# Attention block on one core: q of the twelve plain units given out up to two units sooner, the first quad's y twice a unit

## The chip, the cores and the metric

The kernel runs on one core of a Trainium2 chip. The metric is the device time in microseconds (us), of the slowest core where there are several; here it is the one core. Kernels are compared by medians of runs on the same chip.

The engines are named as in the profile: PE is the matrix engine (TensorE), PEld its weight loads, DVE is VectorE, ACT is ScalarE, POOL is GpSimd, SP is the engine from which all the DMAs of the main part are issued. Each engine takes its instructions strictly in the order in which the program lists them.

## What is computed

A block with adaptive layer norm, attention with 32 query heads over 8 key/value heads and the last 512 positions of a cache, and a gated feed-forward part. Cut to what matters here (the feed-forward part comes after the stretch that the change touches):

```python
def _A_ref(x, k_cache, v_cache, wq, wo):
    W = min(4096, max(256, Sk // 4))          # 512
    q = (x @ wq).reshape(B, Sq, Hq, Dh)       # 2048 rows, 32 heads of 128
    k = jnp.repeat(k_cache[:, :, Sk - W:, :], rep, axis=1)
    v = jnp.repeat(v_cache[:, :, Sk - W:, :], rep, axis=1)
    scores = jnp.einsum("bhqd,bhkd->bhqk", q, k) * (Dh ** -0.5)
    p = _softmax(scores, axis=-1)
    o = jnp.einsum("bhqk,bhkd->bhqd", p, v)
    return o.reshape(B, Sq, Hq * Dh) @ wo

mod = (_silu(c) @ w_mod).reshape(c.shape[0], 6, 1, -1)
h = _layernorm(x, axis=-1) * (1 + ca) + sa
x = x + ga * _A_ref(h, A_k_cache, A_v_cache, A_wq, A_wo)
h = _layernorm(x, axis=-1) * (1 + cb) + sb
x = x + gb * _B_ref(h, B_w_gate, B_w_up, B_w_down)
```

## The kernel before

**Precision.** Every float32 operand of a product is split into two float16 halves, a high and a low one, and each product is three matmuls (low by high, high by high, high by low) into one float32 bank: the helper `mm3` at L91 issues nearly all the matmuls of the program. A split is made in two instructions: the high half as a copy with a cast (on ACT or POOL), the low half as the difference (on DVE or POOL).

**Units and steps.** The attention goes by units: one head of one block of 512 query rows. Four units (two heads by two row blocks) form a group g, which shares one pair of heads `pr`; two pairs share one key/value head (a quad of heads). A unit has four steps t, each for 128 query rows: unit u holds steps 4u to 4u+3. A step of the main loop issues, in this order:

- PE: the scores `ps` of step t, three matmuls, into one of two banks (a third score tile can start only when the exponential of two steps before has read its bank);
- DVE: the row maximum `nm` of `ps`; ACT: the exponential `ee` from `ps` and `nm` into a tile of its own, with the row sums;
- ACT: the high half `p` of step t-2; DVE: the low half `p` of step t-3, behind which SP issues the DMA that turns both halves (`pt<-p`, a DMA transpose);
- PE: up to three groups of three matmuls, popped from a list `work`, or from a second list `ywork` when the first is empty.

Step 0 is the first `ps` of the profile; the steps below are counted by the groups of three `ps` matmuls.

**What the lists hold.** At the first step of each unit u, `pushes(u, y)` adds to `work`: the product of probabilities and V of unit u-2 (`po`, four groups, which need all four turned tiles of unit u-2), the q product of a coming unit, and, from unit 12 on, output products `y` (`py`: o by wo of a finished quad of heads, four groups for 128 rows, added to the running sum by DVE). For the first three groups of units (g < 3, units 0 to 11, "plain") q of unit u+1 is one product of four groups (`pq`). From g = 3 on the q of a group of four units is made by a scheme with seven products instead of eight (`qa`, `qb`, `qc`), spread over the four units before; its operands are combinations of the weights, which POOL makes as a set (`w0`, `w1`, `w2`, `x3`). Where a step finds both lists empty, PE has only the three `ps` matmuls there.

**Small work with a due step.** Loads, statistics and weight preparation are put on a table by step. `sched(pos, (load, steps))` sets the step at which a preparation runs and lets its load be issued up to three steps sooner, when its buffer is free; `at(("w", t), fn)` runs a function at the end of step t. A pair of weight tiles `rw` goes through two buffers (`NRW` = 2): the next pair's load waits until the previous pair has been converted. For each pair of weights ACT takes a sum of squares (`junk<-rw`), PE sums it over the partitions (`pst`), and POOL and DVE make scales of it; K has the same statistic (`junk<-raw`). Plain weights of the third pair are split by ACT and DVE, those of the second pair by POOL. These statistics stand in ACT's list between the exponentials.

**Where the change is.** `turned_out`, `get_qt` and `yt_turn` take tiles from the ring "qt"; the loop over g at L1233 and below sets the due steps; `pushes` builds the PE list; the main loop at its end adds `y`. The number of buffers of "qt" is written as 3 in three places.

Of the kernel before, what the change touches and what calls it, by code (L numbers as in the profile page):

```python
# [48 lines left out]
GW = 3  # L49
# [3 lines left out]
NPT = 3  # L53
NE = 6
CB = (11, 27)
PSE = dict.fromkeys((5, 7, 8, 9, 14, 18, 19, 21, 22, 23, 25, 26, 27), "acc") | dict.fromkeys((11, 15, 20, 24, 28), "qa")
# [9 lines left out]
def block_kernel(ctx: ExitStack, tc: tile.TileContext, x, kT, v, wq, wo, wg, wu, wd, cT, wc, wm, out):  # L66
# [500 lines left out]
    def turned_out(qb, dt):  # L567
        tag, n = (("qt", 3), ("v16", 2))[dt % 2]
        f = pool.tile([P, D], F32, tag=tag, name="hf", bufs=n)
        v = f.rearrange("p (t q) -> p t q", t=QT)  # L570
        sc = cols[:, 4, dt:dt + 1]
        nc.scalar.activation(v, TURN[qb][:, :, dt, :], AF.Identity, scale=sc, bias=cols[:, 3, dt:dt + 1])
        put_off(2, lambda: nc.vector.scalar_tensor_tensor(v, TURN[qb][:, :, KT + dt, :], sc, v, op0=ALU.mult, op1=ALU.add))
        put_off(4, lambda: dma(spilled(3, qb)[:, dt, :], f))
# [59 lines left out]
    def get_qt():  # L634
        return pair("qt", "qt", 3)

# [598 lines left out]
    for g in range(NG):  # L1235
# [6 lines left out]
        if 0 < g < GW:  # L1242
            a, b = plain_steps(g, by)
            sched_pair(g, srcs, t0 - (19 if g > 1 else 13), spread, [(t0 - (12 if g > 1 else 8), a)], [(t0 - (8 if g > 1 else 7), b)])
        elif g >= GW and (not half or pr < GW):
# [14 lines left out]
        else:  # L1260
            if g > 0:
                if pr % 2 == 0:
                    load, stat, spread_, parts = k_items(pr)
                    sched(t0 - (22 if g > 2 else 20), (load, [stat]))
                    at(("w", t0 - (19 if g > 2 else 17)), spread_)
                load, stat, spread_, parts = k_items(pr)
# [284 lines left out]
    def pushes(u, y):  # L1551
# [11 lines left out]
        if g < GW:  # L1563
            w = q_plain(u + 1) if 0 < u + 1 < 4 * GW else []
            if u + 1 == 4 * GW:
                return nxt[2] + nxt[6] + pv + nxt[7]
            return w + pv + (nxt[1] if nxt and k == 2 else [])
        f = items(g)
# [9 lines left out]
    with tc.manual_schedule():  # L1578
        begin()
        nexty, invs = [], {}  # L1580
        for t in range(T + TAIL):
            now[0] = t
            u, s = divmod(t, 4)
            if s == 0:
# [3 lines left out]
                work += pushes(u, y)  # L1588
            if s == 2 and (t >= T or u < GW * 4) and nexty:
                ywork += nexty.pop(0)  # L1590
# [137 lines left out]
    def yt_turn(g, c, qb):  # L1728

        def split():  # L1730
            tag, bufs = (("qt", 3), ("v16", 2))[YR.get("n", 0) % 2]
            u = YR["u", c, qb] = pool.tile([P, 2, QB], U16, tag=tag, name="yu", bufs=bufs)
# [128 lines left out]
```

## Time and profile before

| | us |
|---|---|
| median of 3 runs | 1726.62 |
| lowest and highest | 1725.72, 1727.48 |
| span of the profiled execution | 1724.3 |
| PE busy in it | 1705.4 |
| DVE busy | 1424.2 |
| ACT busy | 1257.4 |
| POOL busy | 1088.1 |

The span runs from the first to the last instruction of one profiled execution. The time of that execution is not listed apart; the difference of its span to the median of the runs is 2.3 us, for what lies before the first and behind the last instruction.

How the views are read: the page gives the busy time of each engine. The list of waits says which engine waited for whom, in total, how often, and the longest. The table of windows gives, for a stretch of the span, the busy time of PE, PEld, DVE, ACT and POOL with the count of instructions, the clock granted to PE, the busy share of the DMA engines and their GB/s. The timeline gives the start, the length, the engine, the line, the operation and what it writes and reads, a count, and in square brackets the idle time before it. The end of a matmul is modelled: a single one is shown as 0.38 us long while the next may start much sooner, so PE's pace is read from starts. SPq rows are DMAs as SP issues them; the length is that of the issue, and the list of DMA issues says how long after the issue they land.

### The profile page before, as it was taken

The numbers are of one execution on the slowest core, as the hardware profiler recorded it, in microseconds if no ns is written. First come the engines' busy times: TensorE is split into PE (matmuls) and PEld (weight loads), VectorE is DVE, ScalarE is ACT, GpSimd is POOL, SyncE is SP. The second block draws the span as 40 slices with busy tenths as digits, with TensorE's granted clock in tenths as the row PEclk, the third lists the DMA queues.
The fourth block names the chain that finished last, engine by engine and source line by source line (L and its number), as shares of the span: only waits on it lengthen the run. The fifth ranks groups of instructions, "written<-read, shape, count | busy, mean of one in ns | idle before, by whom it ended". The sixth has DMA issues, their size and how long they took to land.

```text
span 1724.3 us, 26250 instructions
## 1 busy us (share of the span) xinstructions
PE 1705.4 (99%) x7961; PEld 780.0 (45%) x7961; DVE 1424.2 (83%) x2480; ACT 1257.4 (73%) x2823; POOL 1088.1 (63%) x1322
## 2 busy tenths in 40 slices
PE   7999999999999999999999999999999999999999
PEld 4344444444444444444444444444444444444444
DVE  8888888888888999888888888888896788676666
ACT  7988788888878877888778777788785354455442
POOL 3879777776788884655665755757760345735424
PEclk9999999999999999999999999999999999999999
DMA  7999999999999998999999999899997556365353
GB/s 242 222 207 214 214 217 205 226 202 227 213 217 236 201 212 181 212 211 225 216 220 222 211 227 206 198 236 212 222 232 162 164 144 195 121 165 174 99 158 102
DMA packets 693454, 343.51 MB, mean 199 GB/s; under 512 B 579136, under 2 KB 602688, under 8 KB 693312
## 3 DMA queue, kind: packets, MB, share of 16 engines
q1 hardware_dynamic: 693024, 341.30, 85.3%
q8 instruction: 63, 1.03, 0.3%
q14 instruction: 79, 0.65, 0.1%
q10 hardware_dynamic: 288, 0.52, 0.1%
HBM read 137.50 MB, written 63.70 MB: 117 GB/s over the span
## 4 chain that ended last, share of the span: by engine, by line
PE 92%; ACT 4%; DVE 2%; DMA 2%; issue 1%; SPq 0%; ACTq 0%; DVEq 0%
PE py L91 20%; PE po L91 18%; PE ps L91 17%; PE fa L91 8%; PE qa L91 8%; PE fc L91 4%; PE qc L91 4%; PE ya L91 4%; PE qb L91 2%; PE fb L91 2%; PE yc L91 2%; ACT ee L1009 1%; ACT p L1021 1%; PE yb L91 1%; DMA rw<-in_wq 1%
## 5 line engine op out<-in xcount | busy, mean ns | idle before, releaser
L1009 ACT ACTIVATE ee<-ps,nm 128x512 f32<-128x512 f32 x512 | 349.7, 683 | 185.3 <-DVE nm L1000 182.7
L1026 DVE SCALAR_TENSOR_TENSOR p<-ee,rr,p 128x512 f16<-128x512 f32 x512 | 454.4, 888 | 8.5 <-ACT p L1021 8.0
L1000 DVE TENSOR_REDUCE nm<-ps 128x1 f32<-128x512 f32 x512 | 350.1, 684 | 96.8 <-PE ps L91 94.9
L91 PE MATMUL ps<-k,qt 128*128 128x512 f16 x1536 | 414.7, 379 | 4.4 <-ACT ee L1009 3.3
L1021 ACT ACTIVATE p<-ee,rr 128x512 f16<-128x512 f32 x512 | 363.9, 711 | 16.5 <-DVE rr L1017 11.8
L91 PE MATMUL po<-pt,v 128*128 128x512 f16 x1536 | 372.9, 379 | 2.1 <-DMA pt<-p 0.8
L91 PE MATMUL py<-wo,ot 128*128 128x512 f16 x1536 | 371.3, 379 | 0.0
L91 PEld LDWEIGHTS <-w 128*128 128x128 f16 x2184 | 213.4, 98 | 259.6 <-issue 2.0
L91 PEld LDWEIGHTS <-v 128*128 128x128 f16 x1536 | 149.8, 98 | 184.6 <-issue 3.0
L91 PEld LDWEIGHTS <-ot 128*128 128x128 f16 x1536 | 150.3, 98 | 181.2
L91 PEld LDWEIGHTS <-qt 128*128 128x128 f16 x1536 | 145.7, 98 | 178.0 <-issue 6.0
L1337 POOL TENSOR_TENSOR fg<-fg 128x512 f32<-128x512 f32 x48 | 62.9, 1311 | 135.8 <-DVE fg L1311 133.0
L754 DVE SCALAR_TENSOR_TENSOR ot<-po,ot 128x512 f16<-128x512 f32 x128 | 87.8, 686 | 40.4 <-ACT ot L753 39.9
L1321 ACT ACTIVATE at<-fg 128x512 f16<-128x512 f32 x92 | 56.3, 626 | 77.8 <-DVE fg L1311 61.0
L1009 ACT ACTIVATION_READ_ACCUMULATOR ee<-ps,nm 128x1 f32 x512 | 100.1, 196 | 0.0
L970 DVE SCALAR_TENSOR_TENSOR acc<-py,ysc,acc 128x512 f32<-128x512 f32 x128 | 94.7, 739 | 5.3 <-PE py L91 5.3
L91 PE MATMUL qa<-t,w 128*128 128x512 f16 x348 | 84.9, 379 | 0.0
L91 PE MATMUL fa<-t,w 128*128 128x512 f16 x336 | 81.7, 379 | 0.1
L237 POOL TENSOR_TENSOR lw<-lw,half__86 128x1 f32<-128x1 f32 x38 | 25.9, 681 | 85.7 <-DVE lw L188 85.6
L753 ACT ACTIVATE ot<-po 128x512 f16<-128x512 f32 x128 | 73.9, 578 | 5.0 <-PE po L91 5.0
L404 POOL TENSOR_TENSOR rs<-rs,nhalf 128x1 f32<-128x1 f32 x32 | 18.5, 577 | 93.7 <-DVE rs L398 85.8
L91 PEld LDWEIGHTS <-wo 128*128 128x128 f16 x504 | 49.3, 98 | 59.7 <-issue 0.5
(258 smaller groups left out, 2802.9 us busy)
## 6 DMA issues: line engine op xcount, KB each, us to landing
w<-kept SPq DMA_DIRECT2D x123, 256.0 KB, 3.3
wo<-kept SPq DMA_DIRECT2D x72, 256.0 KB, 3.2
kept<-stage SPq DMA_DIRECT2D x67, 256.0 KB, 3.0
raw<-in_wo SPq DMA_DIRECT2D x56, 256.0 KB, 3.2
kept<-w SPq DMA_DIRECT2D x39, 256.0 KB, 3.0
rw<-in_wq SPq DMA_DIRECT2D x38, 256.0 KB, 3.1
hs<-hf SPq DMA_DIRECT2D x32, 256.0 KB, 2.9
pt<-p SPq DMA_TRANSPOSE x512, 3.4
```

The source lines that it names most:

```text
L91: nc.tensor.matmul(ps, a, b, start=first and n == 0, stop=last and n == 2, skip_group_check=chain)
L237: nc.gpsimd.tensor_tensor(out, out, half_, op=ALU.pow)
L404: nc.gpsimd.tensor_tensor(st["rs"], st["rs"], nhalf, op=ALU.pow)
L753: nc.scalar.activation(t[:, 0, :], src, AF.Copy, scale=scale)
L754: return lambda: nc.vector.scalar_tensor_tensor(t[:, 1, :], src, scale, t[:, 0, :], op0=ALU.mult, op1=ALU.subtract)
L970: nc.vector.scalar_tensor_tensor(acc[ti], st["p"], by, acc[ti], op0=ALU.mult, op1=ALU.add)
L1000: nc.vector.tensor_reduce(nm, E[t]["ps"], axis=AX.X, op=ALU.max, negate=True)
L1009: nc.scalar.activation(e, E[t]["ps"], AF.Exp, bias=E[t]["nm"], scale=1.0, accum_out=sm[:, t % 2:t % 2 + 1])
L1021: nc.scalar.activation(p16[:, 0, :], E[t]["e"], AF.Copy, scale=E[t]["r"])
L1026: nc.vector.scalar_tensor_tensor(p16[:, 1, :], E[t]["e"], E[t]["r"], p16[:, 0, :], op0=ALU.mult, op1=ALU.subtract)
L1321: nc.scalar.activation(t[:, 0, :], g, AF.Copy)
L1337: nc.gpsimd.tensor_tensor(g[o], g[a], g[b], op=ALU.subtract)
```

## The change

It does five things.

1. The ring "qt" has five buffers (`NQT`) where it had three.
2. A table `QAT` says which units' q are given out in which unit: unit 1's in unit 0, 2's in 1, 3's in 2, then those of 4 and 5 in unit 3, 6 and 7 in 4, 8 in 5, 9 and 10 in 6, 11 in 7. Before, it was always unit u+1's in unit u. The first of a unit's q stands ahead of `po`, the second behind it.
3. The third pair's weights (g = 2): the sum of squares is due three steps sooner (22 steps ahead of the group's first step for 19), the split of the first tile 15 for 12, of the second 13 for 8.
4. K's statistic for the second key/value head (g = 2) is due three steps sooner.
5. In units 8 to 11 `y` is added to the second list at the first step of a unit too, not only at the third.

```diff
+NQT = 5
+QAT = ((1,), (2,), (3,), (4, 5), (6, 7), (8,), (9, 10), (11,))
...
-        tag, n = (("qt", 3), ("v16", 2))[dt % 2]
+        tag, n = (("qt", NQT), ("v16", 2))[dt % 2]
...
-        return pair("qt", "qt", 3)
+        return pair("qt", "qt", NQT)
...
-            sched_pair(g, srcs, t0 - (19 if g > 1 else 13), spread, [(t0 - (12 if g > 1 else 8), a)], [(t0 - (8 if g > 1 else 7), b)])
+            sched_pair(g, srcs, t0 - (22 if g > 1 else 13), spread, [(t0 - (15 if g > 1 else 8), a)], [(t0 - (13 if g > 1 else 7), b)])
...
-                    sched(t0 - (22 if g > 2 else 20), (load, [stat]))
-                    at(("w", t0 - (19 if g > 2 else 17)), spread_)
+                    sched(t0 - (22 if g > 2 else 23), (load, [stat]))
+                    at(("w", t0 - (19 if g > 2 else 20)), spread_)
...
-            w = q_plain(u + 1) if 0 < u + 1 < 4 * GW else []
+            w = [q_plain(n) for n in (QAT[u] if u < len(QAT) else ())]
             if u + 1 == 4 * GW:
                 return nxt[2] + nxt[6] + pv + nxt[7]
-            return w + pv + (nxt[1] if nxt and k == 2 else [])
+            return (w[0] if w else []) + pv + (w[1] if len(w) > 1 else []) + (nxt[1] if nxt and k == 2 else [])
...
-            if s == 2 and (t >= T or u < GW * 4) and nexty:
+            if (s == 2 and (t >= T or u < GW * 4) or s == 0 and u in (8, 9, 10, 11)) and nexty:
                 ywork += nexty.pop(0)
```

The third place of "qt", in `yt_turn`, changes as the first.

Which instructions stand where is the same on every engine up to step 8 and again from step 64 on; between them the following moves. In numbers of PE's matmuls (`ps` counted in): steps 8 to 11 hold 36 before and after, steps 12 to 29 hold 168 before and 204 after, steps 30 to 47 hold 216 both times, steps 48 to 63 hold 186 before and 150 after. Both kernels have the same matmuls in sum.

**ACT, steps 9 to 12.** Here `p` with a number is the high half of one step, `ee` the exponential, `junk<-wor` the sum of squares of a wo tile, `junk<-raw` that of K, `junk<-rw` that of a weight tile. Before, from the q copy of step 9 on:

```order
L753 ACTIVATE qt<-pq,qsc 128x512
L220 ACTIVATE junk,lm<-wor 128x512
L1009 ACTIVATE ee,sm<-ps,nm 128x512
L1021 ACTIVATE p_711<-ee,rr 128x512
L753 ACTIVATE ot<-po 128x512
L1009 ACTIVATE ee,sm<-ps,nm 128x512
L1014 ACTIVATE rr<-sm 128x2
L1021 ACTIVATE p_743<-ee,rr 128x512
L1009 ACTIVATE ee,sm<-ps,nm 128x512
```

and after, from the same copy on:

```order
L755 ACTIVATE qt<-pq,qsc 128x512
L222 ACTIVATE junk,lm<-wor 128x512
L222 ACTIVATE junk,lm<-raw 128x512
L1011 ACTIVATE ee,sm<-ps,nm 128x512
L1023 ACTIVATE p_715<-ee,rr 128x512
L755 ACTIVATE ot<-po 128x512
L222 ACTIVATE junk,lm<-rw 128x512
L1011 ACTIVATE ee,sm<-ps,nm 128x512
L1016 ACTIVATE rr<-sm 128x2
L1023 ACTIVATE p_749<-ee,rr 128x512
L222 ACTIVATE junk,lm<-rw 128x512
L1011 ACTIVATE ee,sm<-ps,nm 128x512
```

Three sums of squares, one of K and two of weight tiles that have to be loaded first, now stand ahead of the exponentials of steps 10, 11 and 12; before, they stood behind them, in steps 12 to 14.

**SP, the loads of the same place.** `raw<-in_kT` loads a K tile, `rw<-in_wq` a weight tile, `u<-hs` and `cb` tiles of the layer norm; `pt<-p` with a number is the turn of one step. Before, from the fourth wo tile on:

```order
L97 DMA wor<-in_wo 128x512
L1030 DMA_TRANSPOSE pt<-p_585 128x8x128
L97 DMA raw<-in_kT 128x512
L1030 DMA_TRANSPOSE pt<-p_621 128x8x128
L1030 DMA_TRANSPOSE pt<-p_644 128x8x128
L97 DMA u_689<-hs_1_473 128x512
L97 DMA raw<-in_kT 128x512
L1030 DMA_TRANSPOSE pt<-p_675 128x8x128
L97 DMA cb<-hs_1_473 128x512
L97 DMA rw<-in_wq 128x512
L1030 DMA_TRANSPOSE pt<-p_711 128x8x128
L97 DMA rw<-in_wq 128x512
```

and after:

```order
L99 DMA wor<-in_wo 128x512
L99 DMA raw<-in_kT 128x512
L1032 DMA_TRANSPOSE pt<-p_585 128x8x128
L99 DMA raw<-in_kT 128x512
L1032 DMA_TRANSPOSE pt<-p_623 128x8x128
L1032 DMA_TRANSPOSE pt<-p_646 128x8x128
L99 DMA u_691<-hs_1_473 128x512
L99 DMA rw<-in_wq 128x512
L1032 DMA_TRANSPOSE pt<-p_677 128x8x128
L99 DMA cb<-hs_1_473 128x512
L99 DMA rw<-in_wq 128x512
```

One K load moves ahead of a turned tile, the first weight load stands where the second K load stood, and the second weight load where the first weight load stood.

**PE, steps 51 to 54, and 58 to 60.** Of a group of equal matmuls the first row is shown; weight loads are left out; the counts are in the text. `w` with a number is a weight tile, the `w` of `qa<-b` being that of the fifth pair (g = 4), `v` the second half of V. Before, from the `ps` of step 51 to the first `qa<-b` of the fifth pair:

```order
L91 MATMUL ps<-k,qt 128x512
...
L91 MATMUL po<-pt,v_1547 128x512
...
L91 MATMUL py<-wo,ot 128x512
...
L91 MATMUL ps<-k,qt 128x512
...
L91 MATMUL qc<-t_207,w_1671 128x512
...
L91 MATMUL py<-wo,ot 128x512
...
L91 MATMUL ps<-k,qt 128x512
...
L91 MATMUL py<-wo,ot 128x512
...
L91 MATMUL ps<-k,qt 128x512
...
L91 MATMUL qa<-b_201,w_1985 128x512
```

and after, from the `ps` of step 51 to the same `qa<-b`:

```order
L93 MATMUL ps<-k,qt 128x512
...
L93 MATMUL py<-wo,ot 128x512
...
L93 MATMUL ps<-k,qt 128x512
...
L93 MATMUL qc<-t_207,w_1717 128x512
...
L93 MATMUL qa<-b_201,w_2029 128x512
```

From the `ps` of step 48 to this `qa<-b` PE had 75 matmuls before, and has 51 after (steps 48 to 50 twelve each, step 51 six, and three `ps` and six `qc` of step 52). On POOL, which makes that weight tile, the order in this stretch is the same as before, from the scale of the third V tile (`vmax<-vmax`) on.

Before, from the `ps` of step 58 to the first `po` of step 60:

```order
L91 MATMUL ps<-k,qt 128x512
...
L91 MATMUL py<-wo,ot 128x512
...
L91 MATMUL po<-pt,v_1547 128x512
...
L91 MATMUL ps<-k,qt 128x512
...
L91 MATMUL po<-pt,v_1547 128x512
...
L91 MATMUL ps<-k,qt 128x512
...
L91 MATMUL qa<-t_205,w_2116 128x512
...
L91 MATMUL po<-pt,v_1547 128x512
```

and after:

```order
L93 MATMUL ps<-k,qt 128x512
...
L93 MATMUL po<-pt,v_1595 128x512
...
L93 MATMUL ps<-k,qt 128x512
...
L93 MATMUL qa<-t_205,w_2148 128x512
...
L93 MATMUL po<-pt,v_1595 128x512
```

The last `po` of each piece is the first that needs the turned tiles of steps 52 to 55. From the `ps` of step 58 to it there were 33 matmuls, and there are 21 now: the `y` that stood between is gone to steps 33 to 43, and step 59 has nothing but its `ps`.

More of the change, by code (lines that the diff above doesn't have):

```diff
@@ L1730, in split @@
         def split():
-            tag, bufs = (("qt", 3), ("v16", 2))[YR.get("n", 0) % 2]
+            tag, bufs = (("qt", NQT), ("v16", 2))[YR.get("n", 0) % 2]
             u = YR["u", c, qb] = pool.tile([P, 2, QB], U16, tag=tag, name="yu", bufs=bufs)
```

## The prediction

> **What bounds the kernel now.** I read the page first, then PE's list of waits.
>
> ```profile
> span 1724.3 us, 26250 instructions
> PE 1705.4 (99%) x7961; PEld 780.0 (45%) x7961; DVE 1424.2 (83%) x2480; ACT 1257.4 (73%) x2823; POOL 1088.1 (63%) x1322
> ```
>
> PE is busy for 99% of the span, and the change adds and removes no matmul. So it can only move waits of PE. PE's list of waits for 33 to 97 us (engine and line waited for, total, times, longest) has these on top:
>
> ```profile
> PE ps L91 <- ACT ee L1009: 3.0, 4, 1.3
> PE po L91 <- DMA pt<-p: 0.8, 1, 0.8
> PE po L91 <- DVE lw L188: 0.5, 1, 0.5
> ```
>
> Idle time in that list hides a little, because the ends of matmuls are modelled. I measure waits by PE's pace instead. PE's timeline gives the pace, and the starts of steps 12, 13, 30:
>
> ```profile
> 53.08 0.81 PE L91 MATMUL ps<-k,qt 128*128 128x512 f16 x3 [1.29 <-ACT ee L1009]
> ...
> 55.67 0.81 PE L91 MATMUL ps<-k,qt 128*128 128x512 f16 x3
> ...
> 93.15 1.46 PE L91 MATMUL po<-pt,v 128*128 128x512 f16 x6 [0.85 <-DMA pt<-p]
> 94.44 0.81 PE L91 MATMUL ps<-k,qt 128*128 128x512 f16 x3
> ...
> 97.70 2.10 PE L91 MATMUL py<-wo,ot 128*128 128x512 f16 x9
> 99.64 0.81 PE L91 MATMUL ps<-k,qt 128*128 128x512 f16 x3
> ```
>
> Nine matmuls take 99.64 - 97.70 = 1.94 us, 0.2156 each. Steps 12 to 29 take 94.44 - 53.08 = 41.36 us and hold 168 matmuls, 36.22 us. The 5.1 us over that are waits (0.1 of it short sums). Behind step 30 PE is busy throughout. The table of windows (PE, PEld, DVE, ACT, POOL busy; clock; DMA) shows who sets the pace:
>
> ```profile
> 63.00:97.00 34.00, 30.89 (x139) 13.15 (x138) 28.51 (x56) 32.55 (x80) 26.49 (x34) 1.00 1.02 214
> 97.00:130.00 33.00, 33.00 (x157) 15.03 (x156) 29.03 (x53) 26.81 (x63) 26.52 (x39) 1.00 0.93 217
> ```
>
> Up to 97 us ACT is busy 96% of the time and PE stops for it wherever a step has nothing but its scores; behind that PE is full and ACT has room. The whole prize is 5 us in 1724, 0.3%.
>
> **What the change takes away.** Steps 12 to 29 now hold 204 matmuls, 44.0 us, 2.44 us a step. ACT had 32.55 us of work in 34 us, so 0.957 of a step of 41.36 / 18 = 2.30 us: 2.20 us a step. With three more q copies in the stretch it stays near 2.3 us. PE becomes the longer of the two, and its waits for `ee` go. Its waits for turned tiles go too, where full steps now stand ahead of `po`; I keep 0.3 us for two places with a light step ahead (steps 25 and 57). Old waits: -5.0 us.
>
> **What it adds, first: sums of squares ahead of exponentials (steps 10 to 14).** ACT's timeline, SP's, and the landing times of the DMAs issued from 51 to 56 us (size, median us to landing):
>
> ```profile
> 51.64 0.63 ACT L220 ACTIVATE junk<-wor 128x512 f16<-128x512 f32 x1
> ...
> 52.25 0.69 ACT L1009 ACTIVATE ee<-ps,nm 128x512 f32<-128x512 f32 x1
> ...
> 53.48 0.61 ACT L753 ACTIVATE ot<-po 128x512 f16<-128x512 f32 x1
> 53.96 0.68 ACT L1009 ACTIVATE ee<-ps,nm 128x512 f32<-128x512 f32 x1
> ```
>
> ```profile
> 51.65 0.40 SPq L97 DMA_DIRECT2D raw<-in_kT  x1
> ...
> 55.27 0.39 SPq L97 DMA_DIRECT2D rw<-in_wq  x1
> ```
>
> ```profile
> raw<-in_kT SPq DMA_DIRECT2D x1, 256.0 KB, 4.3
> ...
> rw<-in_wq SPq DMA_DIRECT2D x1, 256.0 KB, 3.8
> ```
>
> K's sum comes ahead of the exponential of step 10: 52.25 - 51.64 = 0.61 us, and PE's 53.08 becomes 53.7. Next, ACT reaches the first weight tile's sum at 53.96 + 0.61 = 54.6. That tile is now loaded from the place of the K load at 51.65, about 0.5 us later because one more load stands ahead, and lands 4.3 us on, near 56.4. So the next exponential starts near 57.0 for 53.96, and PE, which followed the last one 53.08 - 52.25 = 0.83 us after its start, has `ps` of step 13 at 57.85. It is ready for it at 53.7 + 12 x 0.2156 = 56.3: 1.5 us lost. Bounds: 0.6 if it lands as fast as the 3.8 row without the delay ahead, 3.4 at the 6.0 us of the slowest weight load before. The second weight tile keeps the place at 55.27 and lands near 59.1, when ACT is there; 0.1 us. Sum: 0.6 + 1.5 + 0.1 = 2.2 us.
>
> **Second: the set of the fifth pair (step 52).** PE's `qa` of that pair comes after 51 matmuls from step 48 on, for 75. It needs the tile that POOL has written last at 154.56:
>
> ```profile
> 111.30 0.57 POOL L237 TENSOR_TENSOR vmax<-vmax,half__86 128x1 f32<-128x1 f32 x1 [2.78 <-DVE vmax L186]
> ...
> 154.56 1.61 POOL L162 TENSOR_TENSOR w<-rw,w 128x512 f16<-128x512 f32 x1
> ```
>
> ```profile
> 110.06 0.81 PE L91 MATMUL ps<-k,qt 128*128 128x512 f16 x3
> ...
> 157.37 1.46 PE L91 MATMUL qa<-b,w 128*128 128x512 f16 x6
> ```
>
> ```profile
> 112.00:156.00 44.00, 44.00 (x207) 20.03 (x206) 37.92 (x65) 35.20 (x85) 41.06 (x51) 1.00 0.95 208
> ```
>
> POOL waits for DVE at 111.30, 1.2 us after PE's step 36 began (110.06), and is then busy 41.06 of 44 us, without a gap that the timeline shows: a chain of its own from step 36 to 156.17, 46.1 us. PE takes (144 + 51) x 0.2156 = 42.0 us to the same point; before it was 47.3. So PE stands there for 4.1 us. Lower bound 1.1, if the 2.9 us between POOL's instructions closed up; upper 5, if as many of POOL's instructions as 1.16 against 1.61 us for the same form fall long. I take 4.1, the row itself. A short wait of step 48 (ACT's copy of `qa`, half a microsecond) comes out of it, not on top.
>
> **Third: turned tiles of steps 52 to 55 (step 60).**
>
> ```profile
> 167.11 0.81 PE L91 MATMUL ps<-k,qt 128*128 128x512 f16 x3
> ...
> 174.23 0.81 PE L91 MATMUL po<-pt,v 128*128 128x512 f16 x3
> ```
>
> ```profile
> 170.32 1.24 SPq L1030 DMA_TRANSPOSE pt<-p  x1
> ```
>
> ```profile
> pt<-p SPq DMA_TRANSPOSE x5, 3.1
> ```
>
> DVE's low half of step 55 stands in step 58, as before; SP issued its turn 170.32 - 167.11 = 3.2 us after PE began step 58, and it lands 3.1 us later (165 to 176 us). That is 6.4 us after the step began, with the semaphore about 6.5. PE came after 7.1 us; with 21 matmuls it comes after 4.5. It waits 2.0 us; 1.0 to 3.0 as the landing goes. Other light steps (56, 60, 64) I count at nothing: there ACT's sum is 35.20 of 44 us, not 96%. If that cover is gone they cost as much as before, 0.5 to 0.9 us each.
>
> **The sum.** -5.0 + 0.3 + 2.2 + 4.1 + 2.0 = +3.6 us. The span 1724.3 would be 1727.9. The runs' median is 2.3 us over this span, and I carry that: 1726.6 + 3.6 = **1730.2 us**. Five buffers for q cost nothing: the ring only frees earlier.
>
> **The rivals.** *A, the forecast*: three waits come back behind the five microseconds that go. From 1728.6 to 1732. For it: the places are fixed by order, and two of three prices are differences of measured starts. Chance 0.45.
>
> *B, the clock falls*: the same, and the wait of 4.1 us lets PE's clock down.
>
> ```profile
> 12.80:16.10 3.30, 0.91 (x6) 0.53 (x7) 2.32 (x13) 2.54 (x7) 0.19 (x1) 1.00 1.05 393
> 16.20:19.50 3.30, 3.30 (x9) 0.93 (x8) 2.98 (x11) 3.00 (x6) 1.86 (x3) 0.50 0.26 97
> ...
> 50.00:53.10 3.10, 1.81 (x10) 0.70 (x8) 1.90 (x4) 3.07 (x10) 2.85 (x5) 1.00 1.11 241
> ```
>
> After 3.3 us in which PE was busy for 0.91, the clock was 0.50 for the next 3.3; after 1.81 of 3.10 it stayed. A wait of 4.1 us leaves some 3.3 us emptier than the first of these rows in most positions. Price: half of 3.3 us, 1.65, so 1731.9. Against it: one such case in the trace, at the start. Chance 0.23. The Trainium skill, page "TensorE: Matmul & The Clock Gate", section "What's actually happening", says that the clock goes to half after at least one idle window of about 3.4 us, on windows that run freely. By that a wait of 4.1 us would have to cover a whole window, which it does in about one position of five, an estimate by that page. The row of 12.80 disagrees in part: there 28% busy was enough.
>
> *C, not slower*: POOL's chain doesn't hang on step 36 but starts as early as in the old time, and the set is there. It decides when POOL's `vmax` starts 4 us before PE's step 36 plus 1.2. Price: -4.1, so 1726.1. For it: POOL had idle time ahead (2.78 us). Against it: that idle time ended with DVE, whose place is fixed. Chance 0.20, a quarter of it with the load of step 13 early as well and so faster.
>
> *D, light steps cost as before*: 0.6 us at each of three places, 1732; or the change doesn't do what it says, since the third pair's weights, made in steps 17 to 20 for steps 20 and 24, come late and q waits for them. Chance 0.12.
>
> **How the numbers follow.** About 0.2%, 3.5 us, is what a measurement of this kernel can tell from no change, and +3.6 lies on that edge. A splits 0.24 slower, 0.21 same; B 0.23 slower; C 0.15 same, 0.05 faster; D 0.10 slower, 0.02 same. Slower 0.57, same 0.38, faster 0.05. The range takes in B and D with the upper bounds of the first wait, and C down to its middle: 1726.8 to 1734.0.
>
> **What would show it.** Steps 16 to 29 without waits, and step 30 beginning near 99.6 us (94.44 + 36 x 0.2156 - 2.6). A wait of near 4 us ahead of `qa` at step 52, named for POOL; one of 2 us ahead of `po` at step 60, named for a DMA; ACT idle near 55 us for `rw`. Wrong would be: POOL's tile ready before PE comes; `ps` of step 13 by 56.5; a clock below 1 behind step 52 speaks for B.

## The result, and the profile after

The changed kernel takes 1739.5 us (median of 5 runs, 1738.2 to 1742.3), against 1726.65 us before (1725.7 to 1727.5): ratio 1.0078, 95% interval 1.0066 to 1.0090. It is 12.9 us slower; the forecast was 3.6 us slower, with a range that ended at 1734.0 us. Of all the runs in this document one is left out, the profiled execution of e7, which took 2369.9 us at a mean granted clock of 0.71. The first lines of the page of the changed kernel:

```profile
span 1737.7 us, 26245 instructions
PE 1707.4 (98%) x7961; PEld 780.2 (45%) x7961; DVE 1430.7 (82%) x2480; ACT 1258.8 (72%) x2823; POOL 1085.5 (62%) x1322
```

PE does the same 7961 matmuls in a span 13.4 us longer. PE's list of waits for 33 to 195 us (engine and line, what it waited for; total, times, longest) says where they stand:

```profile
PE po L93 <- DMA pt<-p: 6.3, 4, 3.1
PE ps L93 <- ACT ee L1011: 4.6, 4, 2.0
PE qa L93 <- POOL w L164: 3.1, 1, 3.1
PE pq L93 <- DVE qt L756: 0.9, 1, 0.9
```

The waits for `ee`, which were to go, are longer than before (3.0 us for 33 to 97 us there). Those for turned tiles have grown from 0.8 us, and two others have come.

To place them I take PE's timeline step by step: the time from a step's first `ps` to the next step's, less 0.2156 us for each of its matmuls of 512 columns (0.03 for a small one). What is left is waiting, or a clock below full. By this measure, in us:

| steps | before | after | after, second profile | forecast for after |
|---|---|---|---|---|
| 8 to 13 | 2.5 | 4.3 | 4.7 | 4.2 |
| 14 to 21 | 1.6 | 0.0 | 0.0 | 0 |
| 22 to 31 | 3.0 | 3.1 | 3.0 | 0.3 |
| 32 to 45 | 0.0 | 3.7 | 2.8 | 0 |
| 46 to 55 | 0.0 | 4.1 | 6.1 | 4.1 |
| 56 to 63 | 0.0 | 5.0 | 5.4 | 2.0 |
| sum | 7.1 | 20.1 | 22.0 | |

(4.2 is 2.5, less the 0.5 of step 13 that counted as an old wait, plus 2.2. The second profile is run e14 below.) The sum grows by 13.0 us, which is the whole result (12.9 us by the medians). From step 64 on both kernels run alike to 0.7 us. So the gap has to be explained at four places: steps 22 to 31, 32 to 45, 46 to 55, 56 to 63.

**Steps 22 to 31.** PE waits 2.0 us in steps 22 to 24 and 1.0 us in step 26. PE's timeline of the changed kernel shows the two main places; DVE's, ACT's and POOL's of the same stretch follow (start, length, instruction, idle time before it):

```profile
85.44 0.81 PE L93 MATMUL ps<-k,qt 128*128 128x512 f16 x3 [1.25 <-ACT ee L1011]
...
93.88 0.81 PE L93 MATMUL pq<-y,w 128*128 128x512 f16 x3 [0.87 <-DVE qt L756]
```

```profile
78.60 1.63 DVE L1028 SCALAR_TENSOR_TENSOR p<-ee,rr,p 128x512 f16<-128x512 f32 x1
80.16 1.75 DVE L756 SCALAR_TENSOR_TENSOR w<-rw,wsc,w 128x512 f16<-128x512 f32 x1
81.84 0.68 DVE L1002 TENSOR_REDUCE nm<-ps 128x1 f32<-128x512 f32 x1
82.44 0.74 DVE L1028 SCALAR_TENSOR_TENSOR p<-ee,rr,p 128x512 f16<-128x512 f32 x1
```

```profile
82.55 0.66 ACT L1011 ACTIVATE ee<-ps,nm 128x512 f32<-128x512 f32 x1 [1.83 <-DVE nm L1002]
```

```profile
78.53 1.16 POOL L387 TENSOR_TENSOR t<-u,t 128x512 f16<-128x512 f32 x1
79.65 1.72 POOL L665 TENSOR_TENSOR wor<-wor,gs 128x512 f32<-128x512 f32 x1
```

PE began `ps` of step 21 at 78.52, so DVE could have taken its maximum `nm` near 79.3. It did so at 81.84, behind a `p` of 1.63 us and a weight split `w` of 1.75 us. The same `p` takes 0.74 in the fourth row. Both slow ones began while an instruction of POOL ran (78.53 to 79.69, 79.65 to 81.37), and both ended 0.54 us behind its end, at 80.23 and 81.91: as if they had stood until POOL was done. ACT was idle for 1.83 us, and PE's `ps` of steps 23 and 24 waited for its exponentials. ACT then worked on until 93.5 us with only 0.29 us of idle time. Its part of the q copy that PE waits for in step 26 came late in that queue, at 92.36; that this wait has the same cause is argued from these rows. The same two splits of the third pair's weights before the change:

```profile
76.46 0.75 DVE L754 SCALAR_TENSOR_TENSOR w<-rw,wsc,w 128x512 f16<-128x512 f32 x1 [0.38 <-ACT w L753]
...
84.77 1.23 DVE L754 SCALAR_TENSOR_TENSOR w<-rw,wsc,w 128x512 f16<-128x512 f32 x1
```

They took 0.75 and 1.23, and the change moves them sooner, to another place beside POOL's work.

**Steps 32 to 45.** PE's timeline:

```profile
107.50 0.81 PE L93 MATMUL ps<-k,qt 128*128 128x512 f16 x3
109.21 2.10 PE L93 MATMUL po<-pt,v 128*128 128x512 f16 x9 [0.91 <-DMA pt<-p]
111.15 0.81 PE L93 MATMUL ps<-k,qt 128*128 128x512 f16 x3
```

In units 8, 9 and 10 no q is left to stand ahead of `po`. So `po` follows straight behind `ps`, 15 matmuls or 3.2 us sooner in its unit than before, and waits: 1.1, 1.9 and 0.65 us at steps 32, 36 and 40.

**Steps 46 to 55.** POOL's timeline and PE's:

```profile
150.09 0.64 POOL L243 TENSOR_SCALAR kmax<-kmax 128x1 f32<-128x1 f32 x1
153.63 0.55 POOL L239 TENSOR_TENSOR lw<-lw,half__86 128x1 f32<-128x1 f32 x1 [2.91 <-DVE lw L190]
...
166.53 1.15 POOL L164 TENSOR_TENSOR w<-rw,w 128x512 f16<-128x512 f32 x1
```

```profile
163.14 1.46 PE L93 MATMUL qc<-t,w 128*128 128x512 f16 x6
167.74 0.82 PE L93 MATMUL qa<-b,w 128*128 128x512 f16 x3 [3.14 <-POOL w L164]
```

PE waits for POOL where the forecast had it, 3.3 us at step 52. The 0.3 at step 46 and 0.5 at step 48 are of another kind: at step 48 PE's list names ACT's copy for `qa`, and in the second profile at step 46 too.

**Steps 56 to 63.** PE's timeline, SP's, and the table of windows around the wait at step 52 (first two) and that at step 60 (last two); the number behind POOL's count is the granted clock:

```profile
182.02 1.46 PE L93 MATMUL qa<-t,w 128*128 128x512 f16 x6
...
186.60 1.46 PE L93 MATMUL po<-pt,v 128*128 128x512 f16 x3 [3.12 <-DMA pt<-p]
```

```profile
181.04 1.23 SPq L1032 DMA_TRANSPOSE pt<-p  x1
...
182.36 0.71 SPq L99 DMA_DIRECT2D rw<-in_wq  x1
...
183.17 1.23 SPq L1032 DMA_TRANSPOSE pt<-p  x1
```

```profile
164.40:167.70 3.30, 0.20 (x1) 0.00 (x0) 1.53 (x4) 1.89 (x6) 3.13 (x5) 1.00 1.12 184
167.70:171.00 3.30, 3.26 (x16) 1.50 (x17) 1.75 (x3) 1.00 (x4) 2.97 (x5) 1.00 1.05 261
...
183.20:186.50 3.30, 0.28 (x2) 0.00 (x0) 3.08 (x5) 2.20 (x6) 3.13 (x4) 1.00 1.07 247
186.60:189.90 3.30, 3.30 (x8) 1.19 (x9) 2.45 (x4) 2.48 (x6) 3.13 (x4) 0.50 0.73 182
```

The wait for the turned tile is 3.3 us, and behind it the clock is at half for 3.3 us, which costs 1.7 us more. Behind the wait at step 52, just as long, it stays full.

### The profile page after: what moved, and what is told of

The parts are those of the page before. It is cut to its first block, busy times and chain, and to the rows that moved or that the text cites. A ratio compares the mean times of both kernels' runs of the same rounds, so it can differ in the third digit from the quotient of the medians.

```text
span 1737.7 us, 26245 instructions
## 1 busy us (share of the span) xinstructions
PE 1707.4 (98%) x7961; PEld 780.2 (45%) x7961; DVE 1430.7 (82%) x2480; ACT 1258.8 (72%) x2823; POOL 1085.5 (62%) x1322
## 4 chain that ended last, share of the span: by engine, by line
PE 86%; ACT 5%; DVE 4%; DMA 3%; POOL 1%; issue 1%; SPq 0%; POOLq 0%; DVEq 0%; ACTq 0%
PE py L93 19%; PE po L93 17%; PE ps L93 16%; PE fa L93 8%; PE qa L93 8%; PE fc L93 4%; PE qc L93 4%; PE ya L93 3%; PE qb L93 2%; PE fb L93 2%; DMA pt<-p 2%; PE yc L93 2%; ACT ee L1011 1%; ACT p L1023 1%; DVE p L1028 1%
## 5 line engine op out<-in xcount | busy, mean ns | idle before, releaser
L1028 DVE SCALAR_TENSOR_TENSOR p<-ee,rr,p 128x512 f16<-128x512 f32 x512 | 459.8, 898 | 8.1 <-ACT p L1023 7.6
L406 POOL TENSOR_TENSOR rs<-rs,nhalf 128x1 f32<-128x1 f32 x32 | 18.4, 576 | 92.9 <-DVE rs L400 84.9
L1709 DVE SCALAR_TENSOR_TENSOR yt<-ya,dyc,yt 128x512 f32<-128x512 f32 x82 | 60.3, 746 | 19.4 <-PE ya L93 19.4
```

The costliest lines, as they stand in the source:

```text
L1028: nc.vector.scalar_tensor_tensor(p16[:, 1, :], E[t]["e"], E[t]["r"], p16[:, 0, :], op0=ALU.mult, op1=ALU.subtract)
L1709: nc.vector.scalar_tensor_tensor(YT[key], ps, by, YT[key], op0=ALU.mult, op1=ALU.add)
```

## The experiments

Each run was timed beside runs of the kernel before on the same chip; their medians were 1726.1 to 1727.1 us. The table gives the median time, and sums the waits of steps 8 to 63 as above, from one profiled execution of each run; "clock" is the part of them that comes from matmuls starting 0.43 us apart instead of 0.2156. For e7 no waits are given.

| run | what differs | time, us | waits | clock |
|---|---|---|---|---|
| before | | 1726.65 | 7.1 | 0 |
| after | | 1739.5 | 20.1 | 1.7 |
| e14 | after, once more | 1741.0 (one run) | 22.0 | 3.4 |
| e1 | after, y once a unit | 1736.55 | 18.4 | 1.7 |
| e2 | after, y ahead of po | 1737.7 | 18.5 | 2.9 |
| e3 | after, two wo parts later on POOL | 1738.8 | 18.9 | 1.7 |
| e4 | after, weights' sums a step later | 1740.1 | 20.6 | 4.7 |
| e5 | after, y once and ahead of po | 1734.8 | 14.6 | 1.5 |
| e6 | after, light steps 22, 23 filled | 1742.4 | 22.8 | 6.7 |
| e7 | e5, lighter steps spread out | 1730.1 | | |
| e8 | e7, sums a step later | 1729.4 | 9.1 | 0 |
| e9 | before, y twice only | 1730.7 | 12.1 | 1.7 |
| e10 | before, weights and K's sum sooner only | 1733.5 | 13.2 | 3.3 |
| e11 | e5, V's parts sooner | 1732.8 | 13.7 | 0 |
| e12 | e5 with several remedies | 1729.6 | 9.2 | 0 |
| e13 | after, light steps elsewhere | 1742.3 | 21.1 | 3.3 |

**One part alone: e9 and e10.** From the kernel before:

```diff
-            if s == 2 and (t >= T or u < GW * 4) and nexty:
+            if (s == 2 and (t >= T or u < GW * 4) or s == 0 and u in (8, 9, 10, 11)) and nexty:
```

> The kernel before with y twice in units 8 to 11 and nothing else: no matmul leaves the steps up to 63, none of these has fewer than 12 except 63, but the fifth pair's first products stand at step 52 as in the changed kernel. Theory S (the order itself is dear at step 52: POOL needs 14.7 us from step 48, PE has 57 matmuls, 12.3 us): 2.4 us of wait there, none over 0.7 at step 60, the early waits as before (7.1): 1729 to 1730. Rival Z (y twice costs only together with the work that is missing): under 0.8 us of new waits, 1726.6 to 1727.3.

It took 1730.7 us (ratio 1.0024, 1.0015 to 1.0033). The wait at step 52 is 2.6 with the start of a fall of the clock in it (2.1 without), at step 48 0.5, at step 60 none, and the early waits are 7.7 for 7.1: theory S. PE's rows:

```profile
156.02 1.32 PE L91 MATMUL qa<-b,w 128*128 128x512 f16 x3 [1.96 <-POOL w L162]
157.13 1.49 PE L91 MATMUL ps<-k,qt 128*128 128x512 f16 x3
```

The new order at step 52 is dear by itself, with every step full. Three `ps` matmuls in 1.28 us instead of 0.65 (the next row began at 158.41) show the halved clock behind the wait. It takes 1.7 us of this execution (1730.1 us); whether it is also what lifts the median over the expected 1730 is not shown.

```diff
-            sched_pair(g, srcs, t0 - (19 if g > 1 else 13), spread, [(t0 - (12 if g > 1 else 8), a)], [(t0 - (8 if g > 1 else 7), b)])
+            sched_pair(g, srcs, t0 - (22 if g > 1 else 13), spread, [(t0 - (15 if g > 1 else 8), a)], [(t0 - (13 if g > 1 else 7), b)])
...
-                    sched(t0 - (22 if g > 2 else 20), (load, [stat]))
-                    at(("w", t0 - (19 if g > 2 else 17)), spread_)
+                    sched(t0 - (22 if g > 2 else 23), (load, [stat]))
+                    at(("w", t0 - (19 if g > 2 else 20)), spread_)
```

> The kernel before with the third pair's weights and K's statistic sooner and nothing else. Theory R (K's sum and the weight tiles' sums stand ahead of exponentials that PE waits for): steps 11 to 13 have 3.5 us of waits or more instead of 1.9, of which up to 0.7 comes back in steps 15 to 17, where the sums stood: 1727.5 to 1728.7, more if the clock falls. Rival N (the sums fill time in which ACT waits anyway): 1726.3 to 1727.

It took 1733.5 us (ratio 1.0043, 1.0031 to 1.0056): theory R, and dearer than it said. Steps 11 to 13 have 3.9 us, for 1.9 before; 1.7 of it is a fall of the clock at step 12, where the changed kernel waits 1.3. At steps 22 to 24 stand 4.8 us (0.9 before), of which 1.7 is a second fall, one that the changed kernel does not have. So the sooner weights alone cost 6.7 us, half as much as the whole change, though with 3.3 us of half clock that the whole change does not have at these steps. PE's longest list entry is the one that the change was to shorten, and DVE has slow rows here too:

```profile
PE ps L91 <- ACT ee L1009: 6.6, 5, 2.0
```

```profile
76.83 1.67 DVE L1026 SCALAR_TENSOR_TENSOR p<-ee,rr,p 128x512 f16<-128x512 f32 x1
78.42 1.64 DVE L754 SCALAR_TENSOR_TENSOR w<-rw,wsc,w 128x512 f16<-128x512 f32 x1
```

K's statistic was not put back alone: scales of the third pair are made from it (`ksc<-lr,kinv`). The sooner q was not tried alone either; it needs the sooner weights.

**Undoing y twice: e1; y ahead of `po`: e2; both: e5.**

```diff
-            if (s == 2 and (t >= T or u < GW * 4) or s == 0 and u in (8, 9, 10, 11)) and nexty:
+            if s == 2 and (t >= T or u < GW * 4) and nexty:
```

> The changed kernel with y once a unit again (q still out sooner). Waits of PE are counted as a step's length less 0.2156 us a matmul. In the changed kernel these are 7.3 us up to step 31, 3.7 at steps 32, 36 and 40 (po waits for turned tiles), 4.0 at steps 46 to 52 (POOL's set), 5.0 at steps 60 and 61. Theory Y (y taken early empties steps 51 to 63): the 4.0 and the 5.0 go, to 0.5 together; the 3.7 stays, since po still comes straight behind ps there; the steps of 6 matmuls that now stand in 33 to 43 add 1 to 3 us; 1731 to 1734 us. Rival Q (PE is early at the set whatever fills the units, because q was made early): the wait for POOL at step 52 stays over 3 us, and the time is 1735 or more.

Half of theory Y held: of the 4.0 us at steps 46 to 52 there are 0.3 left, of the 5.0 at steps 60 and 61 none. But the time, 1736.55, is beyond its 1734, for the reason that rival Q gave, at another place. PE's and POOL's rows:

```profile
131.09 3.54 PE L93 MATMUL po<-pt,v 128*128 128x512 f16 x9 [4.05 <-POOL v L164]
```

```profile
118.54 0.57 POOL L239 TENSOR_TENSOR vmax<-vmax,half__86 128x1 f32<-128x1 f32 x1 [1.27 <-DVE vmax L188]
...
129.88 1.15 POOL L164 TENSOR_TENSOR v<-raw,v 128x512 f16<-128x512 f32 x1
```

POOL makes V's parts in a chain that starts with `vmax` in step 36 and ends 12.5 us later. PE, with fewer matmuls up to step 40, stands there for 4.2 us, and the clock falls behind it.

```diff
-                work += pushes(u, y)
-            if (s == 2 and (t >= T or u < GW * 4) or s == 0 and u in (8, 9, 10, 11)) and nexty:
+                work += (nexty.pop(0) if u in (8, 9, 10, 11) and nexty else []) + pushes(u, y)
+            if s == 2 and (t >= T or u < GW * 4) and nexty:
```

> The changed kernel with y ahead of po in units 8 to 11, where it has po ahead of y; as many matmuls in every stretch. Theory P (po of steps 32, 36 and 40 comes 15 matmuls sooner than before, because no q stands ahead of it): the 3.7 us of waits there go, 0.4 at most left. At step 52, theory L (POOL's chain starts at DVE's lw of step 48, and PE has 51 matmuls, 11.0 us, against some 14.7): 3.3 us of wait as in the changed kernel, or with a short one at step 48 3.8. The chain that the prediction had, from step 36, 46.1 us, would give 4.0 for both together, which this run can't tell apart, and less than 1 if the waits before stayed. 1735.8 us by P. Rival D (turned tiles late because the DMA queues are slow there): po waits all the same, over 2 us in all, and 1738 or more.

Theory P held at its place: steps 32 to 45 have no wait at all. The time fell by less than the 3.7 us, to 1737.7: `qa` now waits 2.2 us for ACT's copy at step 48 and 1.6 for POOL at step 52 (with short ones 4.2 in sum, for 4.0 in the changed kernel), and the wait at step 60 has grown to 3.9, with 2.9 us of half clock behind it.

```diff
-            if s == 2 and (t >= T or u < GW * 4) and nexty:
+            if s == 2 and (t >= T or u < 8) and nexty:
```

> The changed kernel with y once a unit, and ahead of po in units 8 to 11: po and V have their old places in the unit, and everything from step 44 to 61 stands as before. Waits as in the runs ahead (length of a step less 0.2156 us a matmul). Theory Y+P (what costs late is only the y taken early and po at the front): nothing at 32, 36 and 40, nothing over 0.5 at 48 to 61; up to step 31 still 7.3 us; the steps of 9, 3 and 6 matmuls at 34, 35, 38, 39 and 43 cost 2 to 3.5 with the steps behind them, 62 and 63 1.1; sum 10.5 to 12, time 1730 to 1732. Rival Q (q sooner makes PE early at POOL's work whatever stands in the units): over 2 us at steps 40 to 54 for POOL, 1734 or more.

(This line on top of e2.) Steps 32 and 36 wait for nothing, steps 46 to 61 for 0.4 in sum, as Y and P have it; but V from POOL costs 4.4 us at step 41, and 1.5 of clock. 1734.8: rival Q, at V instead of the set.

**POOL's chains: e3 and e11.**

```diff
-WOP = ((23, 24, 26, 27), (10, 12, 16, 17), (-6, -4, 10, 12), (-6, -4, -3, -2))
+WOP = ((23, 24, 26, 27), (10, 12, 22, 24), (-6, -4, 10, 12), (-6, -4, -3, -2))
```

> The changed kernel with two of POOL's four parts of the second wo quad (3.5 us each) moved from steps 48 and 49 to 54 and 56, behind the fifth pair's set. Theory L: from lw of step 48 POOL then needs 14.7 less 7.0, some 7.7 us, PE has 11.0 of matmuls: the wait of 3.3 us at step 52 goes to 0.3 or less, the rest stays (step 60 counts from step 58), 1736.2 us. Rival S (the set waits for DVE and its loads, not for POOL's wo parts): over 2 us of wait stays at step 52 and the time is 1738 or more.

The wait at step 52 shrinks from 3.3 to 0.9, not to 0.3: with POOL's wo parts away, POOL stands idle for DVE, whose reciprocal has its place in step 52.

```profile
156.59 0.19 POOL L243 TENSOR_SCALAR qsc<-lt 128x1 f32<-128x1 f32 x1
161.81 0.27 POOL L243 TENSOR_SCALAR lr<-lr,lu 128x1 f32<-128x1 f32 x1 [5.02 <-DVE lr L269]
```

The time is 1738.8 for 1736.2: the wait at step 60 is 0.3 longer and 0.5 us come at step 57.

```diff
-                    sched(t0 + 1, (load, [stat, spread_, parts]), t0 + 3, t0 + (6 if g > 2 else 5))
+                    sched(t0 + 1, (load, [stat, spread_, parts]), t0 + (3 if g > 2 else 2), t0 + (6 if g > 2 else 4))
```

> The run with y once and ahead of po (1734.8, 14.7 us of waits, of which 4.3 for POOL's v at step 41 and 1.4 of clock behind it), with V's statistic spread and V's parts on POOL one step sooner. Theory V (V comes late because POOL's chain starts with vmax at step 35 or 36, while PE has 24 matmuls fewer to do up to step 41): the wait at 41 shrinks by 1.5 us or more, and without a wait of that length the clock keeps up; 1731.5 to 1733. Rival O (POOL's other work stands ahead of V in any case): over 3.5 us stays, 1734 or more.

(On top of e5.) Theory V: the wait for V goes from 4.4 us to 0.2, no clock falls, 1732.8. What comes instead is a wait of 3.0 us for POOL's set, at step 54.

**The light steps and the sums: e6, e13, e4.**

```diff
-NQT = 5
+NQT, LIGHT = 5, (14, 16, 18, 20)
...
-            for _ in range(4 if t >= T else EARLY[t] if t < len(EARLY) else 3):
+            for _ in range(4 if t >= T else EARLY[t] if t < len(EARLY) else 2 if t in LIGHT else 3):
```

> The changed kernel with two groups of matmuls instead of three taken from the queue in steps 14, 16, 18 and 20, so that the four groups left stand in steps 22 and 23, which have 2 and 0 in the changed kernel; nothing else moves. Theory E (a step of 3 or 9 matmuls costs because ACT needs some 2.2 us for every step; steps of 9 and 12 in turn, 2.27 us, cost nothing): the 3.1 us of waits at steps 22 to 26 go to 0.8 at most, step 30 begins 2.3 us sooner by that; later waits stay, 1737.2. Rival A (ACT's and DVE's amount of work over the stretch sets it, so that the same waits come back in steps 14 to 21): waits of steps 14 to 26 over 2.2 in sum, 1739.

Theory E fell: steps 14 to 26 have 4.5 us (1.7 of it clock), and 1742.4 is, with e13, the slowest time of all. At step 22 `po` now waits 2.5 us, named for DVE's copy of q, and the clock falls there too.

```diff
-QAT = ((1,), (2,), (3,), (4, 5), (6, 7), (8,), (9, 10), (11,))
+QAT = ((1,), (2,), (3,), (4, 5), (6, 7), (8, 9), (10,), (11,))
```

> The changed kernel with QAT's sixth to eighth entries (8, 9), (10,), (11,) instead of (8,), (9, 10), (11,): steps 22 and 23 are full (12 matmuls) and the two light steps, 9 and 3, are 26 and 27; everything else stands where it did. Theory G (the 3.1 us of waits at steps 22 to 26 belong to the two light steps, for which the forecast had no term): less than 0.8 us at steps 20 to 24, and 1.5 to 3 at steps 26 to 30. Theory W (they belong to the third pair's weights, made in steps 17 to 20 on ACT and DVE, which fill those engines just then): 2 us or more stay at steps 22 to 25. Time 1738.5 to 1741 by both.

PE's and DVE's rows:

```profile
86.73 0.81 PE L93 MATMUL pq<-b,w 128*128 128x512 f16 x3 [2.37 <-DVE qt L756]
...
97.09 1.46 PE L93 MATMUL ps<-k,qt 128*128 128x512 f16 x6
98.38 0.81 PE L93 MATMUL pq<-y,w 128*128 128x512 f16 x3
```

```profile
79.72 1.62 DVE L1028 SCALAR_TENSOR_TENSOR p<-ee,rr,p 128x512 f16<-128x512 f32 x1
81.27 1.75 DVE L756 SCALAR_TENSOR_TENSOR w<-rw,wsc,w 128x512 f16<-128x512 f32 x1
82.94 0.68 DVE L1002 TENSOR_REDUCE nm<-ps 128x1 f32<-128x512 f32 x1
```

Theory W, clearly: 2.5 us stay at step 22, and the light pair at steps 26 and 27 costs nothing; the `ps` of two steps run in one piece at 97.09. (PE then comes sooner to step 32, where it waits 2.6 us for 1.1.) The slow split of 1.75 us is there again. It is named a wait for the copy of q here because another instruction of PE meets it first.

```diff
+        late1 = 1 if key == 2 else 0
...
-        pos_a = ([t] if spread else []) + pa
-        pos_b = ([t + 1, t + 3] if spread else []) + pb
+        pos_a = ([t + late1] if spread else []) + pa
+        pos_b = ([t + 1 + late1, t + 3 + late1] if spread else []) + pb
```

> The changed kernel with the third pair's two sums of squares one step later on ACT, its loads where they are. Theory R (ACT stands for the weight tile's load with the next exponential behind it, 1.49 us idle): ACT's idle time for rw goes, and so does the wait of 1.3 us behind step 12; steps 11 to 13 keep 2.4 us or less of waits (3.7 in the changed kernel), step 16 begins 1.2 us sooner, 1738.2 us. Rival A (ACT's amount of work sets these steps, and the load only fills idle time): step 16 begins within 0.4 us of where it does in the changed kernel, 1739.5.

(The loads are asked for one step further ahead, so that they stay where they are.) What R says of ACT is right. The changed kernel's row first, then this one's:

```profile
56.10 0.63 ACT L222 ACTIVATE junk<-rw 128x512 f16<-128x512 f32 x1 [1.49 <-DMA rw<-in_wq]
```

```profile
56.28 0.63 ACT L222 ACTIVATE junk<-rw 128x512 f16<-128x512 f32 x1 [0.34 <-DMA rw<-in_wq]
```

The idle time goes from 1.49 to 0.34 us. But step 16 begins when it did (65.8 for 65.6), because the clock fell behind the wait of step 11, which it had not done in the changed kernel. Nine matmuls that take 1.94 us took 3.3:

```profile
54.41 3.47 PE L93 MATMUL pq<-b,w 128*128 128x512 f16 x9
```

So the time, 1740.1, says nothing for or against the gain. e8 and e12, with K's sum moved too and no fall of the clock, do.

**Putting it together: e7, e8, e12.**

```diff
-            for _ in range(4 if t >= T else EARLY[t] if t < len(EARLY) else 3):
+            for _ in range(4 if t >= T else EARLY[t] if t < len(EARLY) else 2 if t in LIGHT else 3):
```

> The run before the last (y once, ahead of po) with two groups instead of three in thirteen steps from 14 to 41 (14, 16, 18, 20, 24, 26, 28, 30, 32, 34, 36, 38, 41), so that no step up to 61 behind step 13 has fewer than 9 matmuls: the 36 matmuls that are done early are taken out evenly. Theory E: the waits of 22 to 26 and those of the light steps 34 to 43 go; what is left is 4.3 us up to step 13, 1 to 2 in 14 to 54, 1.1 at 62 and 63: 6.5 to 7.5, the same as before the change (7.1), 1726 to 1728. Rival A: the waits come back spread out, 10 or more in sum, 1730 or more.

(On top of e5, LIGHT being the thirteen steps.) 1730.1 (ratio 1.0019, 1.0009 to 1.0029), the time of rival A and not of theory E; how its waits lie is open.

> The run ahead with the third pair's sums of squares and K's one step later on ACT, loads where they are. Theory R: K's sum no longer stands ahead of the exponential that PE waits for behind step 11 (1.45 us of wait instead of 2.18), and ACT no longer stands for the weight tile (1.3 us at step 12 go, as they did with the squares late, where the clock took them back): 2 us less than the run ahead, 4.5 to 5.5 in sum, 1724.5 to 1726, sooner than before the change. Rival: the sums are as dear a step later (1.5 us or more of waits in steps 12 to 16 without a fall of the clock), 1727 or more.

(On top of e7, with the edit of e4, and the same for K.) 1729.4 (ratio 1.0017, 1.0008 to 1.0026): the rival. Steps 11 and 12 have 1.5 us, as before the change, where the changed kernel had 3.5. But 0.9 us of waits come at step 13 and 1.5 at step 15; steps 11 to 15 hold 4.0 in sum, for 3.7 in the changed kernel and 2.1 before. Nothing was gained in these steps by moving the sums; against e7 the time is 0.7 us lower, less than the runs of each spread.

> A try at a version that keeps the gain: y once, ahead of po; two groups in steps 24 to 38 (even ones) and 41; K's and the weights' sums one step later; V's parts one step sooner; one of POOL's wo parts moved from step 49 to 54. From the runs so far: 2.5 us up to step 13, 3.1 at 22 to 26, 0 to 1 at 41 and at 54: 5.6 to 7.5, against 7.1 before the change: 1725.3 to 1727.3. If other waits come back as they did in every run so far, 1728 or more.

(On top of e5: light steps at 24 to 38 and 41, the sums as in e8, V's parts as in e11, one wo part later.) 1729.6 us (ratio 1.0018, 1.0009 to 1.0027), 9.2 us of waits, none behind step 48 of over 1 us. It removes most of what the change brought late, but not the early part (2.9 us at steps 13 and 14, 2.6 at 23 to 27). No version tried is faster than the kernel before.

**The changed kernel again: e14.**

> The changed kernel once more, for what repeats: the same waits to 0.3 us each (7.3 up to step 31, 3.7 at 32, 36 and 40, 4.0 at 46 to 52, 3.3 ahead of po at step 60), while the falls of the clock behind a wait (one of 1.7 us in the first profile, behind the wait at step 60) come at other waits or not at all, if they hang on something that the program doesn't set; if they hang on the waits alone, at step 60 again and nowhere else.

Without the clock's part the sums are 18.4 and 18.7 us: the waits repeat, the largest difference being 0.5 at step 32. The clock does not: it fell behind step 52, which had left it alone in the first profile, and behind step 60 again. The same kernel shows both, so the program alone does not decide.

## Why the prediction was wrong

**What bounds the kernel** was read rightly: PE's busy time is the same but for the clock, and everything is in its waits.

**Old waits, -5.0, of which 0.3 kept: this is one step that failed.** The prediction put it as "PE becomes the longer of the two, and its waits for `ee` go", from ACT's share of busy time over eighteen steps. The old waits did go at steps 14 to 21 (1.6 to 0.0) and 27 to 29 (2.1 to 0.0). But steps 22 to 24 went from 0.9 to 2.0 us, and step 26 from nothing to 1.0. So steps 22 to 31 have 3.1 us, for 3.0 before and 0.3 in the forecast. The average hid an engine that is late at one place: DVE, which has the third pair's weight splits to do there, at up to 1.75 us instead of 0.75. These splits were moved by the change, and the prediction gave them no price. e10 shows that the sooner weights bring 2.2 us and a fall of the clock at steps 22 to 24 without any q being moved (0.9 before; 4.8, less 1.7 of clock), and e13 that the light steps there are not the cause. No run takes the 1.0 us of step 26 apart. That POOL's work is what makes the split slow was read from the rows and not tried. The Trainium skill, page "SBUF — State Buffer", section "Who interferes with whom", says that of a DVE instruction with two inputs in SBUF and a GpSimd instruction that reads SBUF the later one stands until the first is through; the two slow rows, which end 0.54 us behind POOL's, agree with it, others of the same form do not (below).

**Sums of squares, +2.2: right.** Steps 11 to 13 went from 1.9 to 3.7 us, and 0.5 of the 1.9 was an old wait that the forecast had taken away. The tile landed in time for ACT at 56.1 (forecast 56.4), and `ps` of step 13 began at 57.54 (57.85).

**The fifth pair's set, +4.1: the size right by luck, the chain wrong.** The three waits of steps 46 to 52 are 4.0 us, 3.3 of them for POOL. But the chain does not hang on step 36 and 46.1 us of POOL's work; from there it took 48.7. POOL stood idle for 2.9 us at 153.63 until DVE's `lw`, which follows PE's small matmul at the end of step 47. From step 48 on it is 14.8 us (152.97 to 167.74) against 51 matmuls, 11.0 us: 3.8. The forecast's chain would have left 0.7 us at step 52, since PE had lost 3.3 us on the way. e3 shows that POOL's wo parts are in the chain, e9 that the order alone brings the wait.

**The turned tile at step 60, +2.0: mis-sized.** It measured 3.3. The tile was ready 7.8 us after step 58 began (178.78), not 6.5. SP asked for it after 4.4 us instead of 3.2, because in light steps another turn and a load stand close ahead of it in SP's queue. e1, e5 and e9, where steps 58 and 59 are full, have no such wait.

**Not seen at all, +3.7:** the waits of steps 32, 36 and 40. The prediction had the mechanism, `po` after fewer matmuls, and applied it to step 60 alone; for units 8 to 10 the matmuls were only counted (216 both times in steps 30 to 47), without a look at their order within a unit. e2 and e5 show it: with y ahead of `po` these waits are gone.

**Rival B, the clock:** it fell, at step 60 instead of 52, for 1.7 us (forecast 1.65); in the second profile behind both.

In sum: the forecast's 3.6, plus 2.8 for steps 22 to 31, 3.7 for 32 to 40, and 1.3 and 1.7 at step 60, gives 13.1; measured are 13.0 by the waits and 12.9 by the medians.

What the experiments add is why no remedy was worth its size. Taking PE's waits out of steps 12 to 29 takes 36 matmuls, 7.8 us, from the steps behind, and with them the cover of chains on other engines that are timed from a step and not from PE's work: turned tiles, V, the set, the copies. In e1, e2, e3, e5 and e11 the wait that went let PE arrive sooner at the next.

## What to carry to other kernels

Where an engine is full but for a few microseconds, a stretch's average does not say that a wait will go: look for the one instruction whose place makes the waiting engine late, and price every instruction that the change moves, on each engine, in its new neighbourhood. Work taken early is cover taken away later, so for each chain behind it compare the chain's length, from the step where it really starts, with the matmuls that are left. And when work ahead of an instruction goes, look at every place where it goes, not only at the one where the step is light.

## What the runs showed of the hardware

**The clock falls behind short waits, and not each time.** In 15 profiles of this case (e7 left out), from 42 us on, PE's clock was full behind all waits of under 2.0 us, but for one pair (1.7 and 1.4 us with three matmuls between them, e10). Of the 18 waits of 2.0 to 2.7 us, 6 were followed by half clock, and of the 15 of 2.9 to 4.5 us, 12. A fall costs 1.4 to 1.7 us, once 2.9. The wait behind step 11, 2.1 to 2.2 us in eleven profiles, was followed by a fall in four. The windows around it, first of the changed kernel, then of e6:

```profile
50.20:53.50 3.30, 1.39 (x7) 0.52 (x6) 2.12 (x5) 3.27 (x10) 3.13 (x4) 1.00 1.06 246
53.60:57.00 3.40, 2.75 (x13) 1.27 (x13) 1.97 (x4) 1.91 (x5) 2.49 (x4) 1.00 1.00 239
```

```profile
49.80:53.00 3.20, 1.25 (x6) 0.49 (x5) 2.00 (x5) 3.17 (x10) 3.03 (x4) 1.00 1.14 265
53.20:56.50 3.30, 3.30 (x9) 1.13 (x8) 1.95 (x3) 1.92 (x5) 2.39 (x3) 0.50 1.01 238
```

PE was busy for 1.39 us of 3.30 in the one and 1.25 of 3.20 in the other; the clock behind it was 1.00 and 0.50. The waits themselves are equal, 2.18 and 2.20 us. The Trainium skill, page "TensorE: Matmul & The Clock Gate", section "What's actually happening", has windows of about 3.4 us that run freely, so that the same wait can lie differently in them. That the same kernel shows both agrees with it. That the clock falls after an idle window does not: here some six matmuls lay within the 3.4 us ahead of the fall.

**DVE beside POOL.** From 55 to 95 us of the changed kernel, e10 and e13 thirteen of DVE's `p` and `w` took 1.16 to 1.81 us instead of 0.72 to 0.75, and three took 0.87. Each of the thirteen began within 0.6 us of the start of an instruction of POOL and ended 0.5 to 0.6 us behind the end of it. But `p` of 0.73 and 0.74 us also began so, in the changed kernel at 55.26, 0.16 us behind the start of POOL's split of K (55.10 to 56.26). What decides is open.
